# Attention, a SiLU-gated layer and a cosine-gated layer in one kernel: order of stores and loads, place of the sums, and times of two large loads

## The chip, the cores and the metric

The kernel runs on one core of one Trainium2 chip. The metric is the device time of one execution in microseconds (us); the figure for a version is the median of several runs. One further execution was recorded by the hardware profiler, and every row below is read from that one.

## The reference, cut to what matters

Windowed causal attention over 4 batches, 8 heads, 576 positions and head size 64 gives x of 2304 tokens by 512. Two layers follow, all in float32:

```python
x = attn(q, k, v)                       # 2304 x 512
x = (silu(x @ w_gate) * (x @ w_val)) @ w_out      # 512 -> 1536 -> 512
h = x @ w_in2                           # 512 -> 2048
out = (h * cos(h)) @ w_out2             # 2048 -> 512
```

The inputs are 8 bytes wide per element (float64 taken as int64), so each weight has to be turned into float32 on the chip before it is used.

## The kernel before

Each matrix product is made of three matmuls on two-part numbers (a rounded high part and the rest): high by high, high by low, low by high (lines 80 to 82, and 1065 to 1067). So each operand has to be split into `hi` and `lo` first: a cast on ScalarE (ACT) and a subtraction on GpSimd (POOL) or VectorE (DVE).

The program has three stages. In the first, attention runs, and blocks f = 0 to 2 of the first layer's 1536 columns fill gaps of TensorE (PE); their outputs `ye` are stored to `y1d` in DRAM (L270). In the second, the nine blocks f = 3 to 11 run in five groups ([3], [4, 5], ... [10, 11]). A step k is one group's block f on 384 tokens `tb`, and there are 54 steps: six for the first group, twelve for each other. In the third, the second layer runs over 3 parts of 768 tokens by 8 pairs of blocks; each pair is seven products (`prod`, m = 0 to 6) of sums and differences of quarters of tokens and weights, from which four blocks of h are added up (`take`), and rows of the output follow two pairs later.

One step of the second stage does this, engine by engine in this order. PE: 12 matmuls for the gate and 12 for the value of step k (`begin`), then 12 for the output of step k-2 (`second`). ACT: the cast `uh` of step k-1 (L987), SiLU of step k (L978), then whatever `prepare` brings. DVE: the additions to the accumulator `acc` that fall due (L1011, four of them when a group's last block on these tokens is through), `ul` of step k-1 (L989), the product `s` of step k (L980), then `prepare`'s. PSUM has three banks that gate and value take in turn, and five for the output sums.

`prepare(k, count)` runs beside this and makes the weights ready, of both layers. It has three parts. `pipe.scalar` begins `count` items: ACT takes the words of a loaded weight block `st` apart into `cs` (L903, L904). It then casts finished pieces to `hi` (L920 for weights of the first layer, which stay on the chip; L940 for those of the second) and has POOL subtract for `lo` (L921, L941). `pipe.vector` puts float32 together: three operations on DVE (L881 to L883), one on POOL (L885); and for each pair of blocks of `w_in2` it makes four sums of quarters in `sm` (L870 to L873, DVE). `pipe.load` issues the next load of a raw block into `st` (L91, L96) as soon as POOL has let go of its buffer; there are three of these. The pieces of the second layer are not kept: `hi` and `lo` go to DRAM in `wid` and `wod` (L946, L948), and at most three pieces are made in one step, in three buffers each of `sh` and `sl`. These stores are not issued where the piece is made. They are put into a list, and `pipe.start()` of the next step issues them.

All of these DMAs go through SyncE's queue (SP), which issues in program order and waits at each one until its operands are free. So a store that `pipe.start()` issues in step k+1 stands behind the loads of step k.

Before the second stage the program loads `acc` from `y1d`: three loads of up to 768 tokens at L1080, and one of the last 288 tokens at L1086, after the last store of `ye` and ahead of the first `pipe.load()`. At step `CLOSE` (47) whatever is left of the preparation is finished, and the tokens of the third stage's first part are split. At the start of the third stage `load_raw(1)` (L1265) loads the 768 tokens of the second part, 1.5 MB; `make_xt` splits them from pair 2 on. The weights `ws` (L1055) are loaded seven products ahead.

Of the kernel before, what the change touches and what calls it, by code (L numbers as in the profile page):

```python
# [13 lines left out]
ALU = mybir.AluOpType  # L14
# [14 lines left out]
def kernel(  # L29
# [46 lines left out]
    def f32(ap):  # L76
        return ap.bitcast(F32)
# [746 lines left out]
    class Pipe:  # L824
# [3 lines left out]
        def __init__(self):  # L828
            self.todo = []
            for i in range(1, len(groups1)):  # L830
                new = []
                for f in groups1[i]:
                    pool = wa_p if i % 2 else (wa2_p if f == groups1[i][0] else wb_p)
                    for nm, src, col in (("g", w_gate, True), ("v", w_val, True), ("o", w_out, False)):
                        new.append(("w", (i, nm, f), lambda src=src, f=f, col=col: load_stage(src, f, col, stage2), pool))
                old = self.stash(2 * i - 4) + self.stash(2 * i - 3) if i > 1 else []
                self.todo += old[:4] + new + old[4:]
            self.todo += self.stash(6) + self.stash(7)
            self.stages, self.begun, self.ct = [], 0, {}
            self.added = self.done = 0  # L840
            self.logic, self.sums, self.parts, self.outs = [], deque(), deque(), []
            self.kept, self.freed = {}, set()

        def stash(self, p):
# [6 lines left out]
                    ("o", 2 * p, row(2 * p), None), ("o", 2 * p + 1, row(2 * p + 1), None)]  # L851

        def idle(self):
            return self.done == len(self.todo) and not self.outs

        def start(self):
            for fn in self.outs:
                fn()
            self.outs = []

        def load(self):
            while len(self.stages) < min(len(self.todo), self.added + 3):
# [2 lines left out]
        def vector(self):  # L865
            while self.sums:
                n = self.sums.popleft()
                a, b = self.kept.pop(self.todo[n][1]), self.ct[n]
                m = self.kept["m", n] = stash_m.tile([128, 4, 256], F32, tag="sm", name="sm")
                nc.vector.tensor_tensor(out=m[:, 1], in0=b[:, 0:256], in1=b[:, 256:512], op=ALU.add)  # L870
                nc.vector.tensor_tensor(out=m[:, 2], in0=a[:, 0:256], in1=b[:, 0:256], op=ALU.subtract)
                nc.vector.tensor_tensor(out=m[:, 0], in0=m[:, 1], in1=a[:, 0:256], op=ALU.subtract)
                nc.vector.tensor_tensor(out=m[:, 3], in0=a[:, 256:512], in1=m[:, 0], op=ALU.subtract)  # L873
                self.freed.add(n - 1)
                self.parts.extendleft([(n, 3), (n, 2), (n, 1)])
            for n in self.logic:
                kind = self.todo[n][0]
                st, ct = self.stages[n], self.ct[n]
                if wide:
                    ti = ct.bitcast(U32)  # L880
                    nc.vector.tensor_scalar(ct, ct, LEAST_HIGH, GREATEST_HIGH, ALU.max, ALU.min)  # L881
                    nc.vector.tensor_scalar(ti, ti, 3, None, ALU.logical_shift_left)
                    nc.vector.scalar_tensor_tensor(out=ti, in0=st[:, :, 1], scalar=0x80000000, in1=ti,  # L883
                                                   op0=ALU.bitwise_and, op1=ALU.bitwise_or)
                    nc.gpsimd.tensor_tensor(out=ti, in0=ti, in1=st[:, :, 0], op=ALU.add)  # L885
                self.added += 1
                self.stages[n] = None
                if kind == "b":
                    self.sums.append(n)
                else:  # L890
                    self.parts.append((n, 0))
            self.logic = []

        def scalar(self, count, ready):

            for _ in range(count):
                n = self.begun
                if n == len(self.todo) or n >= len(self.stages) or (n >= 5 and n - 5 not in self.freed):
                    break
                ct = self.ct[n] = ct_p.tile([128, 512], F32, tag="cs", name="cs")  # L900
                st = self.stages[n]
                if wide:
                    nc.scalar.activation(out=ct, in_=st[:, :, 1].bitcast(F32), func=AF.Abs, scale=65536.0)  # L903
                    nc.scalar.activation(out=st[:, :, 0], in_=st[:, :, 0], func=AF.Copy, scale=2.0 ** -29)  # L904
                else:
                    nc.scalar.copy(out=ct, in_=st[:, :, 0])
                self.logic.append(n)
                self.begun += 1
            used = 0
            for _ in range(len(self.parts)):  # L910
                n, part = self.parts.popleft()
                kind, key, _, pool = self.todo[n]
                if kind == "w" and not ready(key[0]) or kind != "w" and used == 3:
                    self.parts.append((n, part))
                    continue
                ct = self.ct[n]
                if kind == "w":
                    hi = pool.tile([128, 512], F32R, tag="wh", name="wh")
                    lo = pool.tile([128, 512], F32R, tag="wl", name="wl")
                    nc.scalar.copy(out=hi, in_=ct)  # L920
                    nc.gpsimd.tensor_tensor(out=lo, in0=ct, in1=f32(hi), op=ALU.subtract)  # L921
                    weights[key] = hi, lo
                    self.freed.add(n)
                    self.done += 1
                    continue
                used += 1
                src, w = ct, 512
                if kind == "o":
                    d = wod[key]
                elif part in (1, 2):  # L930
                    src = self.kept["m", n][:, 2 * part - 2:2 * part].rearrange("p s c -> p (s c)")
                    d = wid[key][:, 2 * part:2 * part + 2]
                elif part == 3:
                    src, w, d = ct[:, 256:512], 256, wid[key][:, 6]
                else:
                    d = wid[key][:, 0:2]
                    self.kept[key] = ct
                hi = stash_s.tile([128, 512], F32R, tag="sh", name="sh")[:, :w]
                lo = stash_s.tile([128, 512], F32R, tag="sl", name="sl")[:, :w]
                nc.scalar.copy(out=hi, in_=src)  # L940
                nc.gpsimd.tensor_tensor(out=lo, in0=src, in1=f32(hi), op=ALU.subtract)  # L941

                def out(d=d, halves=(hi, lo), two=kind != "o" and part < 3):
                    for x, t in enumerate(halves):
                        if two:
                            nc.sync.dma_start(out=d[:, :, x], in_=f32(t).rearrange("p (s c) -> p s c", s=2))  # L946
                        else:
                            nc.sync.dma_start(out=d[:, x], in_=f32(t))  # L948
                self.outs.append(out)
                if kind == "o" or part == 3:  # L950
                    self.freed.add(n)
                if part in (0, 3):
                    self.done += 1

    pipe = Pipe()

# [118 lines left out]
    for _ in load0:  # L1075
        pass
    settle()
    for t in range(0, NT - HT, SB):
        e = min(t + SB, NT - HT)
        nc.sync.dma_start(out=acc[:, :, t:e], in_=y1d[:, :, t:e].rearrange("k p t -> p k t"))  # L1080
    i, tb, f = steps[0]
    early = [l1_mms(weights[i, nm, f], *tbs[tb], pl2.tile([128, 512], F32, tag="l2", name="l2")) for nm in ("v", "g")]
    for _ in a_l2(*last[0]):
        flush()
    flush()
    nc.sync.dma_start(out=acc[:, :, NT - HT:], in_=y1d[:, :, NT - HT:].rearrange("k p t -> p k t"))  # L1086
    fa.close()
    cvt.close()
    stage2 = cv.enter_context(tc.tile_pool(name="stage2", bufs=3, side="right", reuse_waits="tile"))
# [13 lines left out]
    def prepare(k, count):  # L1103
        pipe.scalar(count, lambda i: k >= begins[i - 1] + 2)
        pipe.vector()
        pipe.load()

    pipe.load()
    for k in range(K + 1):
        if k < K:  # L1110
            i, tb, f = steps[k]
            while not all((i, nm, f) in weights for nm in "gvo"):
                pipe.start()
                prepare(k, 1)
        late = split(k - 1) if 0 <= k - 1 < K else None
        flush()
# [1 line left out]
            late()  # L1118
        if k == CLOSE:
            while not pipe.idle():  # L1120
                pipe.start()
                prepare(k, 2)
            cv.close()
            xta = pre.enter_context(tc.tile_pool(name="xta", bufs=1, side="right", reuse_waits="tile"))
# [1 line left out]
            load_ws(7)  # L1126
        if k == CLOSE + 1:
            xt_ops = make_xt(0, xta, acc[:, :, 0:SB])
        if k < CLOSE:
            pipe.start()  # L1130
        if k < K:
            begin(k)
        if k < CLOSE:
            prepare(k, 2 if i and k % 2 == 0 and k % 6 != 4 else 1)
        for op in xt_ops[:4]:
            op()
        xt_ops = xt_ops[4:]
# [130 lines left out]
    rows = deque()  # L1268
    bg = deque()
    p7 = None  # L1270
    load_raw(1)
    for k in range(K2 + 2):
        if k >= 2:
            rows += [(k - 2, fi, j) for fi in range(2) for j in range(6)]
        for m in range(7):
# [22 lines left out]
            if m == 1:  # L1298
                load_wo(k - 1 if k else K2)
            s, p = divmod(k, NPAIR)  # L1300
            if m == 3 and s + 1 < NS and p == 2:
                bg += make_xt(s + 1, xta if s % 2 else xtb, raws[s + 1])
            if m == 3 and s + 2 < NS and p == 6:
                load_raw(s + 2)
# [34 lines left out]
```

## Time and profile before

| | us |
|---|---|
| median of 3 runs (1061.98 to 1067.51) | 1065.03 |
| the profiled execution | 1067.15 |
| its span, first to last instruction | 1065.4 |
| PE busy in the span | 1010.7 |
| DVE, ACT, POOL busy | 762.2, 647.6, 485.1 |
| mean granted clock of PE | 0.976 |

A busy PE is not PE at its peak, since matmuls overlap and since the clock is granted in two levels, 2.4 GHz (1.00) and 1.2 GHz (0.50). What counts is where PE has idle time, what released it, and at which clock it went on. The stages are at about 0 to 300, 300 to 675 and 675 to 1062 us of the span.

### The profile page before, as it was taken

The numbers are of one execution on the slowest core, as the hardware profiler recorded it, in microseconds if no ns is written. First come the engines' busy times: TensorE is split into PE (matmuls) and PEld (weight loads), VectorE is DVE, ScalarE is ACT, GpSimd is POOL, SyncE is SP. The second block draws the span as 40 slices with busy tenths as digits, with TensorE's granted clock in tenths as the row PEclk, the third lists the DMA queues.
The fourth block names the chain that finished last, engine by engine and source line by source line (L and its number), as shares of the span: only waits on it lengthen the run. The fifth ranks groups of instructions, "written<-read, shape, count | busy, mean of one in ns | idle before, by whom it ended". The sixth has DMA issues, their size and how long they took to land.

```text
span 1065.4 us, 17549 instructions
## 1 busy us (share of the span) xinstructions
PE 1010.7 (95%) x5796; PEld 949.8 (89%) x5796; DVE 762.2 (72%) x1632; ACT 647.6 (61%) x1438; POOL 485.1 (46%) x553
## 2 busy tenths in 40 slices
PE   7989999999989899898998999899999999999997
PEld 5779999999979899898898899889999889899996
DVE  6897778876148797897796745589766896566664
ACT  5889898984234363453453422387677786686663
POOL 5776577564224474665565532044322452222231
PEclk9999999999989999899999899899999999999999
DMA  5542233312272545555646541566667755575652
GB/s 148 143 112 56 70 72 85 90 29 88 96 248 81 166 150 177 169 178 169 227 122 193 170 149 60 194 221 197 200 218 229 215 185 178 190 244 173 197 178 79
DMA packets 145690, 163.68 MB, mean 154 GB/s; under 512 B 64704, under 2 KB 106688, under 8 KB 145344
## 3 DMA queue, kind: packets, MB, share of 16 engines
q1 hardware_dynamic: 145600, 162.57, 49.3%
q8 instruction: 46, 0.75, 0.3%
q14 instruction: 44, 0.36, 0.1%
HBM read 126.88 MB, written 35.65 MB: 153 GB/s over the span
## 4 chain that ended last, share of the span: by engine, by line
PE 45%; DMA 5%; POOL 3%; DVE 3%; issue 2%; ACT 1%; SPq 1%; POOLq 0%; ACTq 0%; DVEq 0%
PE l L80 8%; PE l L81 8%; PE l L82 8%; PE pm L1065 5%; PE pm L1066 5%; PE pm L1067 5%; POOL cs L885 2%; PE pm L80 2%; PE pm L82 2%; PE pm L81 1%; DMA wid<-sh 1%; POOL sl L941 1%; DMA wod<-sl 1%; DMA wid<-sl 1%; DMA ws<-wid 1%
## 5 line engine op out<-in xcount | busy, mean ns | idle before, releaser
L1189 POOL TENSOR_TENSOR r<-r,c 128x384 f32<-128x384 f32 x96 | 105.5, 1099 | 263.2 <-ACT r L1187 176.4
L80 PE MATMUL pm<-xh,wh 128*128 128x384 f32 (+1 forms) x452 | 152.2, 337 | 2.3 <-ACT s L978 2.3
L81 PE MATMUL pm<-xl,wh 128*128 128x384 f32 (+1 forms) x452 | 146.6, 324 | 0.0
L82 PE MATMUL pm<-xh,wl 128*128 128x384 f32 (+1 forms) x452 | 146.6, 324 | 0.0
L81 PE MATMUL l<-wo,hh 128*128 128x512 f32 x288 | 113.1, 393 | 0.0
L80 PE MATMUL l<-wo,hh 128*128 128x512 f32 x288 | 113.1, 393 | 0.0
L82 PE MATMUL l<-wo,hl 128*128 128x512 f32 x288 | 112.9, 392 | 0.0
L885 POOL TENSOR_TENSOR cs<-cs,st 128x512 uint32<-128x512 uint32 x56 | 81.8, 1465 | 64.6 <-DVE cs L883 50.3
L1065 PE MATMUL pm<-xh,ws 128*128 128x384 f32 x318 | 107.5, 338 | 0.0
L1066 PE MATMUL pm<-xl,ws 128*128 128x384 f32 x318 | 107.4, 338 | 0.0
L1067 PE MATMUL pm<-xh,ws 128*128 128x384 f32 x318 | 107.3, 337 | 0.0
L581 POOL TENSOR_SCALAR e<-e,st 128x256 f32<-128x256 f32 (+1 forms) x144 | 68.5, 487 | 72.3 <-DVE st L576 38.8
L80 PEld LDWEIGHTS pm<-xh,wh 128*128 128x128 f32 x452 | 86.6, 192 | 3.2 <-ACT s L978 3.2
L81 PEld LDWEIGHTS pm<-xl,wh 128*128 128x128 f32 x452 | 86.8, 192 | 0.0
L82 PEld LDWEIGHTS pm<-xh,wl 128*128 128x128 f32 x452 | 86.2, 191 | 0.0
L80 PE MATMUL l<-uh,wh 128*128 128x384 f32 x216 | 75.0, 347 | 11.0 <-DVE acc L1011 10.9
L1179 ACT ACTIVATE a<-c 128x384 f32<-128x384 f32 x96 | 49.8, 518 | 57.7 <-DVE c L1205 57.7
L989 DVE TENSOR_TENSOR ul<-s,uh 128x384 fp32r<-128x384 f32 x54 | 42.7, 791 | 52.9 <-ACT uh L987 52.8
L1184 DVE SCALAR_TENSOR_TENSOR r<-a,r 128x384 f32<-128x384 f32 x96 | 74.4, 775 | 3.3
L1186 ACT ACTIVATE r<-r 128x384 f32<-128x384 f32 x96 | 50.3, 524 | 40.4 <-DVE r L1184 40.4
L82 PE MATMUL l<-uh,wl 128*128 128x384 f32 x216 | 74.2, 343 | 0.0
L81 PE MATMUL l<-ul,wh 128*128 128x384 f32 x216 | 74.2, 343 | 0.0
(199 smaller groups left out, 2934.6 us busy)
## 6 DMA issues: line engine op xcount, KB each, us to landing
ws<-wid SPq DMA_DIRECT2D x168, 256.0 KB, 2.9
wo<-wod SPq DMA_DIRECT2D x48, 512.0 KB, 4.9
st<-in_moe_w_out_dram SPq DMA_DIRECT2D x28, 512.0 KB, 3.6
st<-in_moe_w_in_dram SPq DMA_DIRECT2D x16, 512.0 KB, 4.0
st<-in_moe_w_gate_dram SPq DMA_DIRECT2D x12, 512.0 KB, 3.9
st<-in_moe_w_val_dram SPq DMA_DIRECT2D x12, 512.0 KB, 4.4
wid<-sh SPq DMA_DIRECT2D x24, 256.0 KB, 4.6
wid<-sl SPq DMA_DIRECT2D x24, 256.0 KB, 4.8
```

What stands on the lines that cost most here:

```text
L80: nc.tensor.matmul(out=ps, lhsT=ah, rhs=bh, start=start, stop=False)
L81: nc.tensor.matmul(out=ps, lhsT=ah, rhs=bl, start=False, stop=False)
L82: nc.tensor.matmul(out=ps, lhsT=al, rhs=bh, start=False, stop=stop)
L581: nc.gpsimd.tensor_scalar(e[:, :w], e[:, :w], st[:, 6 + m:7 + m], 1.0, ALU.mult, ALU.mult)
L885: nc.gpsimd.tensor_tensor(out=ti, in0=ti, in1=st[:, :, 0], op=ALU.add)
L1065: nc.tensor.matmul(out=o, lhsT=wh, rhs=xh_, start=start and kk == 0, stop=False, skip_group_check=True)
L1066: nc.tensor.matmul(out=o, lhsT=wh, rhs=xl_, start=False, stop=False, skip_group_check=True)
L1067: nc.tensor.matmul(out=o, lhsT=wl, rhs=xh_, start=False, stop=kk == 1, skip_group_check=True)
L1179: nc.scalar.activation(out=a, in_=h, func=AF.Copy, scale=INV2PI, bias=MAGIC)
L1184: nc.vector.scalar_tensor_tensor(out=r, in0=a, scalar=-C2, in1=r, op0=ALU.mult, op1=ALU.add)
L1186: nc.scalar.activation(out=r, in_=r, func=AF.Abs)
L1189: nc.gpsimd.tensor_tensor(out=r, in0=r, in1=h, op=ALU.mult)
```

## The change

Five things change. The stores of `hi` and `lo` of a step are issued within the same `pipe.scalar`, all `hi` first, then all `lo`, and so ahead of the loads of that step. The four sums of quarters go from DVE to POOL. `acc` is loaded in three equal parts: the first before the second stage as it was, the others in steps 0 and 2, after `begin`. Two items instead of one are begun in every fourth step (from step 8 on: 10 steps) instead of in two of three even steps (14 steps). In the third stage `load_raw(1)` is issued at pair 1, product 3, and `make_xt` of a next part begins at pair 3 instead of 2.

```diff
         def idle(self):
-            return self.done == len(self.todo) and not self.outs
-
-        def start(self):
-            for fn in self.outs:
-                fn()
-            self.outs = []
+            return self.done == len(self.todo)
...
-                nc.vector.tensor_tensor(out=m[:, 1], in0=b[:, 0:256], in1=b[:, 256:512], op=ALU.add)
-                nc.vector.tensor_tensor(out=m[:, 2], in0=a[:, 0:256], in1=b[:, 0:256], op=ALU.subtract)
-                nc.vector.tensor_tensor(out=m[:, 0], in0=m[:, 1], in1=a[:, 0:256], op=ALU.subtract)
-                nc.vector.tensor_tensor(out=m[:, 3], in0=a[:, 256:512], in1=m[:, 0], op=ALU.subtract)
+                nc.gpsimd.tensor_tensor(out=m[:, 1], in0=b[:, 0:256], in1=b[:, 256:512], op=ALU.add)
+                nc.gpsimd.tensor_tensor(out=m[:, 2], in0=a[:, 0:256], in1=b[:, 0:256], op=ALU.subtract)
+                nc.gpsimd.tensor_tensor(out=m[:, 0], in0=m[:, 1], in1=a[:, 0:256], op=ALU.subtract)
+                nc.gpsimd.tensor_tensor(out=m[:, 3], in0=a[:, 256:512], in1=m[:, 0], op=ALU.subtract)
...
-                def out(d=d, halves=(hi, lo), two=kind != "o" and part < 3):
-                    for x, t in enumerate(halves):
-                        if two:
-                            nc.sync.dma_start(out=d[:, :, x], in_=f32(t).rearrange("p (s c) -> p s c", s=2))
-                        else:
-                            nc.sync.dma_start(out=d[:, x], in_=f32(t))
-                self.outs.append(out)
+                for x, t in enumerate((hi, lo)):
+                    if kind != "o" and part < 3:
+                        outs.append((x, d[:, :, x], f32(t).rearrange("p (s c) -> p s c", s=2)))
+                    else:
+                        outs.append((x, d[:, x], f32(t)))
                 if kind == "o" or part == 3:
                     self.freed.add(n)
                 if part in (0, 3):
                     self.done += 1
+            for x, dst, src in sorted(outs, key=lambda o: o[0]):
+                nc.sync.dma_start(out=dst, in_=src)
...
-    for t in range(0, NT - HT, SB):
-        e = min(t + SB, NT - HT)
-        nc.sync.dma_start(out=acc[:, :, t:e], in_=y1d[:, :, t:e].rearrange("k p t -> p k t"))
+
+    def load_acc(s):
+        c = slice(s * SB, (s + 1) * SB)
+        nc.sync.dma_start(out=acc[:, :, c], in_=y1d[:, :, c].rearrange("k p t -> p k t"))
+
+    load_acc(0)
...
-    nc.sync.dma_start(out=acc[:, :, NT - HT:], in_=y1d[:, :, NT - HT:].rearrange("k p t -> p k t"))
...
-        if k < CLOSE:
-            pipe.start()
         if k < K:
             begin(k)
+        if k in (0, 2):
+            load_acc(1 + k // 2)
         if k < CLOSE:
-            prepare(k, 2 if i and k % 2 == 0 and k % 6 != 4 else 1)
+            prepare(k, 2 if i and k % 4 == 0 else 1)
...
-    load_raw(1)
     for k in range(K2 + 2):
...
+            if k == 1 and m == 3:
+                load_raw(1)
-            if m == 3 and s + 1 < NS and p == 2:
+            if m == 3 and s + 1 < NS and p == 3:
                 bg += make_xt(s + 1, xta if s % 2 else xtb, raws[s + 1])
```

## Rows read from the trace of the kernel before

**Rows 1.** The profile's first part: busy time, share of the span, instructions, of PE.
```profile
PE 1010.7 (95%) x5796; PEld 949.8 (89%) x5796; DVE 762.2 (72%) x1632; ACT 647.6 (61%) x1438; POOL 485.1 (46%) x553
```

**Rows 2.** Busy time by stretches: length, PE, PEld, DVE, ACT, POOL, clock, DMA share, GB/s.
```profile
300.00:675.00 375.00, 349.62 (x1908) 345.53 (x1907) 278.67 (x432) 157.85 (x298) 184.38 (x132) 0.95 0.48 155
675.00:1065.00 390.00, 381.15 (x1885) 342.90 (x1884) 270.49 (x453) 268.02 (x533) 120.94 (x104) 0.99 0.61 197
...
685.00:694.00 9.00, 5.94 (x20) 5.69 (x19) 5.01 (x9) 6.72 (x14) 2.62 (x4) 0.62 0.81 296
```

**Rows 3.** Who waited for whom, PE, 290 to 690 us: total, times, longest.
```profile
PE l L80 <- ACT s L978: 12.1, 4, 5.1
PE l L80 <- DVE acc L1011: 10.9, 4, 4.2
PE l L1065 <- DMA ws<-wid: 3.1, 1, 3.1
```

**Rows 4.** Timeline of DVE, products `s` of steps 2, 47, 53: start, us, instruction, idle before.
```profile
315.30 0.56 DVE L980 TENSOR_TENSOR s<-s,l 128x384 f32<-128x384 f32 x1 [0.41 <-PE l L82]
...
633.26 0.56 DVE L980 TENSOR_TENSOR s<-s,l 128x384 f32<-128x384 f32 x1 [3.13 <-PE l L82]
...
671.06 0.56 DVE L980 TENSOR_TENSOR s<-s,l 128x384 f32<-128x384 f32 x1 [3.13 <-PE l L82]
```

**Rows 5.** Who waited for whom, 300 to 675 us, ACT's casts for the stores.
```profile
ACT sh L940 <- DMA wid<-sh: 62.9, 21, 9.0
...
ACT sh L940 <- DMA wod<-sh: 22.3, 5, 9.2
```

**Rows 6.** Timelines of ACT, POOL and SP around one wait, 353 to 375 us.
```profile
353.44 1.13 ACT L940 CAST sh<-sm 128x512 fp32r<-128x512 f32 x2
...
370.07 0.62 ACT L940 CAST sh<-cs 128x512 fp32r<-128x512 f32 x1 [9.01 <-DMA wid<-sh]
...
360.54 3.08 POOL L885 TENSOR_TENSOR cs<-cs,st 128x512 uint32<-128x512 uint32 x2
...
363.64 0.37 SPq L91 DMA_DIRECT2D st<-in_moe_w_gate_dram  x1
364.07 0.50 SPq L946 DMA_DIRECT2D wid<-sh  x1
```

**Rows 7.** Groups by shape, 300 to 632 us (busy, mean ns, idle); last, min/median/max ns.
```profile
L885 POOL TENSOR_TENSOR cs<-cs,st 128x512 uint32<-128x512 uint32 x56 | 81.8, 1465 | 64.6 <-DVE cs L883 50.3 <-issue 5.5 <-ACT s L978 4.5
...
L941 POOL TENSOR_TENSOR sl<-cs,sh 128x256 fp32r<-128x256 f32 x8 | 8.0, 1002 | 9.4 <-DMA wod<-sl 4.9 <-DMA wid<-sl 4.4
...
L882 DVE TENSOR_SCALAR cs<-cs 128x512 uint32<-128x512 uint32 x56 | 43.6, 778 | 1.9
...
L870 DVE TENSOR_TENSOR sm<-cs x8: 410/426/1500, 349.4 to 606.2; 128x256 f32<-128x256 f32 x8
```

**Rows 8.** The profile's DMA issues: count, KB each, median us to landing.
```profile
ws<-wid SPq DMA_DIRECT2D x168, 256.0 KB, 2.9
...
st<-in_moe_w_gate_dram SPq DMA_DIRECT2D x12, 512.0 KB, 3.9
...
wid<-sh SPq DMA_DIRECT2D x24, 256.0 KB, 4.6
```

**Rows 9.** Timelines of SP and ACT where the second stage begins, 282 to 313 us.
```profile
296.63 3.90 SPq L270 DMA_DIRECT2D y1d<-ye  x4
302.84 0.37 SPq L1086 DMA_DIRECT2D acc<-y1d  x1
...
309.01 0.66 ACT L903 ACTIVATE cs<-st 128x512 f32<-128x512 f32 x1 [9.64 <-DMA st<-in_moe_w_gate_dram]
```

**Rows 10.** Timelines of SP, ACT and PE where the third stage begins, 678 to 698 us.
```profile
680.53 0.36 SPq L1265 DMA_DIRECT2D raw<-y2d  x1
...
690.64 0.48 ACT L1215 COPY q<-l 128x384 f32<-128x384 f32 x1 [2.05 <-PE l L1067]
...
697.81 0.44 PE L1065 MATMUL l<-xh,ws 128*128 128x384 f32 x1 [0.46 <-DVE c L1205]
```

More of the change, by code (lines that the diff above doesn't have):

```diff
@@ L840, in __init__ @@
             self.added = self.done = 0
-            self.logic, self.sums, self.parts, self.outs = [], deque(), deque(), []
+            self.logic, self.sums, self.parts = [], deque(), deque()
             self.kept, self.freed = {}, set()
@@ L908, in scalar @@
                 self.begun += 1
-            used = 0
+            used, outs = 0, []
             for _ in range(len(self.parts)):
@@ L1120 @@
             while not pipe.idle():
-                pipe.start()
                 prepare(k, 2)
@@ L1128 @@
             xt_ops = make_xt(0, xta, acc[:, :, 0:SB])
-        if k < CLOSE:
-            pipe.start()
         if k < K:
             begin(k)
+        if k in (0, 2):
+            load_acc(1 + k // 2)
         if k < CLOSE:
-            prepare(k, 2 if i and k % 2 == 0 and k % 6 != 4 else 1)
+            prepare(k, 2 if i and k % 4 == 0 else 1)
         for op in xt_ops[:4]:
```

## The prediction

> **What bounds the kernel now.** The page's first part comes first: PE is busy 95% of the span [rows 1]. The work for PE is the same after the change, so all that can be won is its idle time and its time at the lower clock. The busy time by stretches says where that lies: in the second stage PE idles 375 - 349.6 = 25.4 us and its granted clock is 0.95 on average, which takes (1 - 0.95) x 375 = 19 us away, a part of it while PE idled anyway. The third stage has 8.9 us of idle time, of which the last few are the drain, and a clock of 0.99 [rows 2]. The view of waits names the releasers: PE waited 12.1 us for SiLU on ACT, 10.9 us for the additions to `acc` on DVE, 3.1 us for a load of `ws` [rows 3].
>
> How much is lost in all is read from the pace. From step 47 to step 53 no preparation runs, and `s` comes every (671.06 - 633.26)/6 = 6.30 us. From step 2 to step 53 it takes 355.8 us, and 51 steps at 6.30 are 321.3 [rows 4]. So 34.5 us are lost behind step 2, idle time and low clock together (pot B). Ahead of it lies one wait of 5.1 us [rows 3], with, as an estimate, some 2 us lost to the low clock behind it (in the whole stage 19 us of clock stand beside 25 of idle time): about 7 (pot A). At the start of the third stage lie 3.1 us of waiting and at most (1 - 0.62) x 9 = 3.4 us of clock [rows 2, 3] (pot C). The most that can be won is 34.5 + 7 + 6.5 = 48 us.
>
> Why ACT and DVE are late is in their own waits: ACT's casts waited 62.9 + 22.3 = 85 us for stores of `sh` made a step before [rows 5]. ACT works in order, so `uh` and SiLU stand behind such a cast; DVE's `ul` and `s`, and its additions, stand behind those. One case in full [rows 6]: two casts are made at 353.4. Their stores could go by 355, but SP holds the loads of that step first, and the last of those waits for POOL's two L885, which end at 363.62. The load is issued at 363.64, the first store at 364.07, nine microseconds late. The next cast needs that buffer, waits 9.0 us and runs at 370.07. PE stands still soon after.
>
> **Stores ahead of loads.** Nothing is added but the order. Stores `hi` wait for ACT's casts, stores `lo` for POOL's subtractions, and both come before the L885 for which the loads wait anyway, so the loads lose only SP's time for issuing: up to six stores at the 0.50 us of a row, 3 us [rows 6]. With three loads ahead in flight and 3.9 us to land [rows 8] that lies beside other work; ACT would wait behind it if POOL fell a step behind. A store of `hi` takes 4.6 us to land [rows 8]. Issued right after its cast it is down well before the same place of the next step, 6.30 us later. So pot B loses its main cause. In the case above, a store that leaves nine microseconds sooner ends a wait of 9.0 us to nothing.
>
> **Fewer double steps.** 14 become 10. By the program's order all 56 items still are begun by step 45; the last piece falls into `CLOSE` itself, with one cast that waits for no late store. Before, the last piece was made in step 44. I cost it at 0 to 2 us, taken as 0: step 47 has no other preparation.
>
> **Sums on POOL.** DVE loses 8 x 4 operations; one takes 0.41 us at best and 1.5 us at worst, median 0.43 [rows 7]: about 1.7 us for a pair of blocks, 14 in all. POOL gets them. No row shows such a sum on POOL; the nearest is the 128x256 subtraction, same two inputs, 1.00 us; the 128x512 one of L885 takes 1.47 [rows 7]. Bounds for a pair: 4 x 0.43 = 1.7 (as fast as DVE) and 4 x 1.47 = 5.9; I take 4.0, from the row of the same shape. On average there is room: POOL is busy 184 us of 375 [rows 2], and 184 + 32 = 216 in some 335 would be 65%. In bursts there is little. In steps 16 to 21 the changed program begins 8 items, makes 10 pieces of 512 columns and two of 256, and sums two pairs: 18 x 1.47 + 2 x 1.0 + 8 = 36 us in 6 x 6.30 = 37.8. Steps 27 to 32 come to 35, steps 38 to 43 to 34 by the same count. Behind a sum on POOL's queue stand the L885 of the step, the loads that wait for these, and the next step's `lo`. POOL and DVE also hold each other up: L870 takes 0.41 us alone and up to 1.5 beside POOL, L882 0.78 on average [rows 7]. So I don't give all of pot B back: 27 of 34.5, the remaining 7.5 for the three bursts. Bounds: 15 (stores still decide half of it) to 34.5.
>
> The row of this case has the subtraction at 1.00 us on POOL against 0.43 on DVE [rows 7]. The Trainium skill, GPSIMD Engine Reference, section Engine selection, advises against this very move: elementwise work on two tensors belongs on VectorE, and GpSimd is about twice as slow. By that rule, trace agreeing (2.3 times), a move of elementwise work to POOL costs time; here that would only show if POOL became the bound, which is the third rival below.
>
> **`acc` in three parts.** Before, the last load of `acc` waited for the last `ye` store and was issued at 302.84, and the first raw block got its place in the queue behind it; ACT's L903 waited for that block until 309.01, 9.6 us, with `uh` and SiLU of step 1 behind it [rows 9]. After, the block can be issued when the stores of `ye` have been, at 296.63 + 3.90 = 300.53 [rows 9]. With 3.9 us to land [rows 8] it is there at about 304.4, 4.6 us sooner. PE's wait shrinks from 5.1 to about 0.5, and the clock may stay up. Of pot A I take 6 back (4.5 to 7). The parts loaded in steps 0 and 2 are first added to in steps 5 and 7, more than 20 us later; what they cost is a place ahead of the later raw loads, at two issues nothing that I can price above 1 us.
>
> **Raw tokens later.** At 680.53 the 1.5 MB load goes ahead of the `ws` loads [rows 10], and PE waits 3.1 us for one of them [rows 3]. Without it a `ws` load lands in 2.9 us [rows 8], and it is asked for as soon as the product seven places ahead is through, some 7 us before its own (1.05 us a product, worked out below). So this wait goes. What is next is ACT. A pair has 21 operations on ACT at about the 0.48 us of a row [rows 10], 10 us, and its seven products, six matmuls each, take PE 42/36 x 6.30 = 7.4 us, as long as no output rows lie between (the first two pairs). While PE stood, ACT had work: it waited for PE only 2.05 us [rows 10]. So the matmul at 697.81, which waited for DVE behind ACT [rows 10], can come at most about 2 us sooner, and PE then waits in front of it instead. A wait of that length lowers the clock again. I take 1 of pot C, bounds -2 and 6.5. The load itself comes at pair 1, ahead of `ws` needed some 12 us later, and `make_xt` at pair 3 still ends before pair 8 needs it: nothing.
>
> **The sum.** Against the profiled execution's 1067.15 (a span of 1065.4 and 1.75 around it): 1067.15 - 6 - 27 - 1 = 1033. That execution lies 2.1 us above the median of 1065.03, so on the median's scale the forecast is 1031.
>
> **The rivals.**
>
> Partial relief, 0.17. The stores leave sooner but three buffers are still too few, or a load of the step before holds SP. For it: many stores took more than the median to land, since they go in sixes. Against: 6.30 us between uses. Price: half of pot B stays, 1065 - 6 - 15 - 1 = 1043.
>
> POOL takes ACT's place, 0.13. If pieces and sums run 20% over their rows' means, because POOL and DVE hold each other up more, the three bursts come to 44, 42 and 41 us instead of 37.8: 6 + 4 + 3 = 13 lost, and with the low clock behind each such wait about 20. 1065 - 6 - 34.5 + 20 + 3 (steps 8 to 10) is about 1048.
>
> The same place on the other side, slower than before, 0.03: the changes other than the sums bring some 35 us, and 5 more are needed to be measurably slower, so the 8 groups of sums would have to cost PE 5 us each. The bursts leave about 1.4 us of slack for each group; so a sum would have to take (4.0 + 1.4 + 5)/4 = 2.6 us. The row says 1.00. The time would be about 1071.
>
> The stores don't in fact pass the loads, or another wait of the same length takes their place: about 1062, 0.03.
>
> All of it, pot C too: 1065 - 48 = 1017 to 1022, 0.04.
>
> **How the numbers follow.** The forecast has 0.60, between 1023 and 1039. The range of 1021 to 1048 takes in partial relief and half of the POOL case and leaves about 0.18 out. What a measurement can tell from no change here is about 0.5%, 5 us. Faster: 0.60 + 0.17 + 0.13 + 0.04 = 0.94; the same 0.03; slower 0.03.
>
> **What would show it.** Right: `s` from step 2 to 53 at 6.4 to 6.5 us a step; ACT's wait for `sh` stores under 25 us; L903's first wait near 5 us; no wait for `ws` near 690 but one for DVE in its place, some microseconds later; mean clock near 0.99. The POOL case would show as PE waiting for DVE or ACT whose own chain ends at L870 to L885 on POOL in steps 16 to 21 and 27 to 32. The prediction is wrong if ACT's casts still wait for stores, if a sum on POOL takes over 1.5 us, or if a new wait stands where raw loads are late.

## The result, and the profile after

The changed kernel takes 1025.96 us (median; 1025.35 to 1027.21) against 1064.97 us before: a ratio of 0.9636, with a 95% interval of 0.9609 to 0.9663. It is 39 us faster. The profiled execution took 1027.21 us with a span of 1025.4, 40.0 us less than before's. Its line numbers lie a little lower: L898 is L903 of before, L935 and L936 are L940 and L941, L972 SiLU, L974 the product `s`, L880 POOL's part of the preparation, L1005 the additions to `acc`, L947 the stores of `hi` and `lo`. Every kernel below has its own line numbers, shifted by its edit.

Busy time by stretches, the second and the third stage of the changed kernel (length, PE, PEld, DVE, ACT, POOL, clock, DMA share, GB/s):

```profile
300.00:635.00 335.00, 334.33 (x1910) 333.76 (x1909) 280.58 (x399) 160.12 (x300) 213.81 (x164) 1.00 0.56 178
635.00:1025.00 390.00, 381.79 (x1896) 343.77 (x1894) 272.47 (x455) 268.61 (x534) 119.62 (x104) 0.99 0.61 198
```

The second stage answers to the first line of [rows 2]: PE idles 0.7 us instead of 25.4, its clock is at 1.00 instead of 0.95, and the stage is 40 us shorter. The third stage is what it was, to within 2 us. Who waited for whom, PE, 290 to 690 us, answering to [rows 3]:

```profile
PE l L1059 <- DVE c L1199: 4.0, 2, 3.6
PE l L80 <- ACT s L972: 0.7, 1, 0.7
```

The waits for `acc` and for `ws` are gone. One wait is left, of 3.6 us, at the start of the third stage, where before had 3.1 us for `ws`. The pace, answering to [rows 4], is read from DVE's timeline (steps 2, 47 and 53):

```profile
312.16 0.55 DVE L974 TENSOR_TENSOR s<-s,l 128x384 f32<-128x384 f32 x1
...
595.15 0.56 DVE L974 TENSOR_TENSOR s<-s,l 128x384 f32<-128x384 f32 x1 [2.74 <-PE l L82]
...
632.95 0.56 DVE L974 TENSOR_TENSOR s<-s,l 128x384 f32<-128x384 f32 x1 [3.13 <-PE l L82]
```

Steps 2 to 53 take 320.8 us, where 51 undisturbed steps at 6.30 us take 321.3; before it was 355.8. That is 35.0 of the 40 us. From step 0 to step 2 it is 10.3 us instead of 15.2 (`s` of step 0 at 301.90, before at 300.09): 4.9 more. From step 53 to the end it is 392.5 instead of 394.3: 1.8. The first stage took 1.8 us longer in this execution, which makes up the difference; in the traces of this document `s` of step 0 comes at anything from 296.9 to 302.2 us, so this lies within what that stage varies by.

And the cause that was named, ACT's casts waiting for stores ([rows 5]; 300 to 635 us here):

```profile
ACT sh L935 <- POOL cs L880: 4.8, 5, 1.6
...
ACT sh L935 <- DMA wid<-sh: 1.7, 1, 1.7
```

85 us of such waits became 1.7. How that comes about is seen in the timelines of ACT, then SP, in steps 8 and 9, the place that answers to [rows 6]:

```profile
354.36 1.12 ACT L935 CAST sh<-sm 128x512 fp32r<-128x512 f32 x2
...
360.72 1.14 ACT L935 CAST sh<-cs 128x512 fp32r<-128x512 f32 x2
...
355.36 0.34 SPq L96 DMA_DIRECT2D st<-in_moe_w_out_dram  x1
355.75 1.58 SPq L947 DMA_DIRECT2D wid<-sh  x3
357.43 2.27 SPq L947 DMA_DIRECT2D wid<-sl  x3
360.87 0.37 SPq L91 DMA_DIRECT2D st<-in_moe_w_gate_dram  x1
```

The casts are made at 354.36 and their stores leave at 355.75, right behind a load of the step before that POOL released at 355.36 (its L880 of 353.82 takes 1.51 us). In the kernel before, the same stores left 10.6 us after their casts began; here it is 1.4 us. The next casts run at 360.72 and wait for nothing.

### The profile page after: what moved, and what is told of

It is laid out like the page before. It is cut to its first block, busy times and chain, and to the rows that moved or that the text cites. A ratio compares the mean times of both kernels' runs of the same rounds, so it can differ in the third digit from the quotient of the medians.

```text
span 1025.4 us, 17616 instructions
## 1 busy us (share of the span) xinstructions
PE 997.0 (97%) x5796; PEld 938.7 (92%) x5796; DVE 765.1 (75%) x1600; ACT 648.9 (63%) x1438; POOL 512.6 (50%) x585
## 4 chain that ended last, share of the span: by engine, by line
PE 88%; ACT 6%; issue 2%; DVE 2%; DMA 1%; POOL 1%; SPq 0%; POOLq 0%; ACTq 0%; DVEq 0%
PE l L80 13%; PE l L81 13%; PE l L82 13%; PE pm L80 7%; PE pm L82 7%; PE pm L81 7%; PE pm L1059 5%; PE pm L1060 5%; PE pm L1061 5%; PE pv L658 3%; PE t L591 2%; PE s L523 2%; ACT e L565 2%; PE pq L426 1%; PE s L80 1%
## 5 line engine op out<-in xcount | busy, mean ns | idle before, releaser
L80 PE MATMUL pm<-xh,wh 128*128 128x384 f32 (+1 forms) x452 | 149.9, 332 | 0.0
L880 POOL TENSOR_TENSOR cs<-cs,st 128x512 uint32<-128x512 uint32 x56 | 80.9, 1445 | 55.1 <-DVE cs L878 47.5
L1178 DVE SCALAR_TENSOR_TENSOR r<-a,r 128x384 f32<-128x384 f32 x96 | 76.8, 800 | 3.3
L565 ACT ACTIVATE e<-e,st 128x256 f32<-128x256 f32 (+1 forms) x144 | 68.0, 475 | 9.4 <-DVE st L556 8.6
L80 PE MATMUL l<-uh,wh 128*128 128x384 f32 x216 | 72.9, 337 | 0.0
```

Of the source, the lines that this page charges most:

```text
L80: nc.tensor.matmul(out=ps, lhsT=ah, rhs=bh, start=start, stop=False)
L565: nc.scalar.activation(out=e[:, :w], in_=e[:, :w], func=AF.Exp, bias=st[:, m:m + 1], scale=-1.0, accum_out=st[:, 2 + m:3 + m])
L1178: nc.vector.scalar_tensor_tensor(out=r, in0=a, scalar=-C2, in1=r, op0=ALU.mult, op1=ALU.add)
```

## The experiments

"Lost" below is the time from `s` of step 2 to `s` of step 53, less 321.3 us. Like 321.3, it is read from one profiled execution of each kernel. All ratios are to the kernel before, measured beside it.

| kernel | median us | ratio, 95% | lost, us |
|---|---|---|---|
| before | 1065 | | 34.5 |
| changed | 1025.96 | 0.9636 (0.9609 to 0.9663) | -0.5 |
| changed, again | 1025.46 | 0.9627 (0.9602 to 0.9652) | 0.0 |
| stores_only | 1036.44 | 0.9738 (0.9703 to 0.9774) | 5.7 |
| old_stores | 1048.63 | 0.9851 (0.9813 to 0.9888) | 23.8 |
| sums_dve | 1026.24 | 0.9647 (0.9612 to 0.9682) | 0.6 |
| doubles14 | 1028.27 | 0.9666 (0.9625 to 0.9708) | 0.1 |
| old_acc | 1031.90 | 0.9684 (0.9662 to 0.9707) | 1.6 |
| raw_early | 1024.68 | 0.9629 (0.9603 to 0.9655) | 0.1 |
| sums_twice | 1031.40 | 0.9681 (0.9662 to 0.9699) | 4.4 |
| sums_x3 | 1057.61 | 0.9929 (0.9908 to 0.9951) | 31.9 |
| cast_pool | 1026.23 | 0.9638 (0.9613 to 0.9662) | 0.1 |
| take_first | 1025.86 | 0.9623 (0.9604 to 0.9643) | -0.9 |
| chains_held | 1021.13 | 0.9599 (0.9578 to 0.9621) | -0.4 |

**The order of the stores, alone and alone undone.** stores_only is the kernel before with the first of the five changes alone: the list and `pipe.start()` go, and each step issues its own stores, all `hi` first.

> The kernel before with one edit, the stores issued within their own step; sums on VectorE, 14 double steps, the loads of acc and of the raw tokens as before. Theory A (the order of stores is the cause of nearly all that the second stage lost): the 34.5 us behind step 2 come back almost whole, while the first wait of 5 us and the one for ws near 690 stay; 1032 to 1038 us. Theory B (relief of VectorE and fewer double steps carry a large share, since PE also waited 10.9 us for VectorE's additions): under half comes back, 1045 to 1055 us, with PE still waiting for acc.

1036.4 us, within theory A's range: 28.7 of the 34.5 us come back by the order alone. No run separates the earlier issue from the order `hi` before `lo`. ACT's casts (300 to 660 us) wait 2.3 us for stores instead of 85:

```profile
ACT sh L935 <- DMA wod<-sh: 2.0, 1, 2.0
...
ACT sh L935 <- DMA wid<-sh: 0.3, 1, 0.3
```

Who waited for whom, PE, 290 to 690 us:

```profile
PE l L80 <- ACT s L972: 5.1, 1, 5.1
PE l L80 <- DVE acc L1005: 4.0, 5, 1.5
PE l L1059 <- DMA ws<-wid: 3.4, 1, 3.4
```

The first and third lines are waits that this part doesn't touch. The second is most of what is left of the stage's loss: five short waits for DVE, none over 1.5 us. The other way round, old_stores is the changed kernel with the list and `pipe.start()` put back.

> The changed kernel with the stores put back into a list that the next step issues; the four other edits stay. Theory A: ScalarE's casts wait for stores again, 60 us or more in all, PE waits for SiLU and additions, 1050 to 1060 us. Theory B: the other edits hold what they won, 1035 to 1045 us.

1048.6 us, a little under theory A's range and above theory B's. The waits of ACT's casts, 300 to 670 us, then PE's:

```profile
ACT sh L940 <- DMA wid<-sh: 52.0, 19, 8.6
...
ACT sh L940 <- DMA wod<-sh: 4.9, 4, 3.3
```

```profile
PE l L80 <- DVE acc L1011: 9.4, 6, 3.5
PE pm L80 <- ACT s L978: 4.3, 3, 2.0
PE l L1065 <- DVE c L1209: 4.0, 2, 3.6
PE l L80 <- ACT s L978: 3.6, 3, 2.1
```

The casts wait 57 us instead of 85, and 23.8 us are lost instead of 34.5. So the other changes aren't worth nothing: while the stores are late, they soften it by 10.7 us. This run has them all together, so it doesn't say which of them does it; sums and schedule are the two that take work or double steps from the stage. Theory A holds for the main part, and not for "nearly all".

**Sums and schedule, each undone.** sums_dve writes `nc.vector` for `nc.gpsimd` in the four sums; doubles14 restores `2 if i and k % 2 == 0 and k % 6 != 4 else 1`.

> The changed kernel with the four sums of quarters back on VectorE. Theory A: VectorE has room for 14 us more, 1025 to 1028 us, no wait of PE comes back. Theory B: PE waits for VectorE's additions to acc again in steps 8 to 45, 1032 us or more.

> The changed kernel with the schedule of 14 double steps of before. Theory A: 1025 to 1029 us, pace of s still under 6.4 us a step. Theory B: double steps that follow each other make VectorE and GpSimd late, PE waits 5 us or more, 1034 us or more.

Neither loses anything that can be seen in its trace: 0.6 and 0.1 us behind step 2. Without both, stores_only loses 5.7. That suggests that each covers for the other, but no run undoes just these two: stores_only lacks the parts of `acc` as well, and a kernel that lacks nothing but those (old_acc, below) loses 1.6 us behind step 2. So about 4 us, as much as the five waits for DVE, are left for sums and schedule together. doubles14's median is 2.3 us higher than the changed kernel's and the intervals overlap; its trace is of the fastest of its four executions (1024.33 us), so what the others lost isn't seen.

**How much POOL bears.** Each line of the four sums stands twice in sums_twice, three times in sums_x3; the values are the same.

> The changed kernel with each sum of quarters on GpSimd made twice, so 7 us a pair of blocks. By the count of GpSimd's work in the three bursts (42, 41 and 39 us against 37.8): 8 us lost behind step 2, some low clock, 1033 to 1038 us. If a loss grows from the first microsecond of sums on GpSimd, half of what three times cost (32 us over two added rounds): 1040 to 1043 us.

> The changed kernel with each sum of quarters on GpSimd made three times in a row (the result is the same), so a pair of blocks costs GpSimd about 10.5 us instead of 3.5, which is 2.6 us a sum, the point from which the prediction's slower rival was to decide. By the count of that rival (GpSimd has 1 to 4 us of slack in a burst of six steps): the three bursts come to 49, 48 and 46 us against 37.8, 30 us lost and more by the low clock, 1058 to 1070 us. By the theory that the buffers between GpSimd and PE take up most of it (three raw loads, five cs, three pieces): 1035 to 1050 us.

Once costs nothing, twice 4.4 us, three times 31.9. That isn't a loss that grows in proportion from the first microsecond. It looks like one that begins near the point where POOL's work in a burst of six steps passes the steps' own 37.8 us. The count of the prediction with the durations after (1.45 for 512 columns, 0.96 for 256, 3.5 for a group of sums) gives 35.0, 33.6 and 32.1 us for once, none over; 42.0, 40.6 and 39.1 for twice, 8 us over in sum where 4.4 were lost; for three times 49, 48 and 46, 29 us over where 31.9 were lost, low clock included. So nothing was lost at 85 to 93% of the 37.8 us by this count, and 4.4 us at 103 to 111%; where between them the loss begins wasn't measured. Nor does the count hit the trace. From `s` of step 16 to `s` of step 22, the sums made once, twice and three times (length, PE, PEld, DVE, ACT, POOL, clock, DMA share, GB/s):

```profile
399.56:439.96 40.40, 40.40 (x232) 40.29 (x231) 38.73 (x48) 20.72 (x40) 33.07 (x26) 1.00 0.69 222
396.28:439.14 42.86, 40.60 (x232) 40.28 (x231) 38.46 (x49) 20.52 (x39) 38.63 (x34) 1.00 0.61 196
399.82:449.77 49.95, 41.91 (x226) 40.76 (x225) 38.42 (x48) 20.46 (x40) 44.53 (x43) 0.91 0.53 174
```

POOL is busy 33.1, 38.6 and 44.5 us, 2 to 5 us less than the count has. In the changed kernel it is DVE, at 38.7 of 40.4 us, that is nearer to its limit there. PE's waits in sums_x3 (290 to 690 us) are for DVE, not for POOL itself:

```profile
PE l L80 <- DVE acc L1013: 19.1, 9, 5.1
PE pm L80 <- ACT s L980: 4.2, 2, 2.5
```

Behind them stand ACT's casts, which wait for POOL's sums (300 to 660 us; L873 and L876 are the last of the third and fourth sum):

```profile
ACT sh L943 <- POOL sm L873: 26.1, 6, 8.3
ACT sh L943 <- POOL sm L876: 16.0, 8, 2.4
```

By time, sums_x3 lies half a microsecond below the range expected by that count, and well over the other theory's. sums_twice, at 1031.4 us, lies under the ranges of both theories: the count foretold 1033 to 1038.

**The loads of `acc`.** old_acc restores the loads at L1080 and L1086 of before and drops those of steps 0 and 2.

> The changed kernel with the accumulators loaded before the second stage, the last load behind the last store of ye, as before. If the first wait was caused by that load's place in the queue: PE's wait near 310 us is 5 us again instead of 0.7, with the lower clock behind it, 1030 to 1033 us. If the raw block would have landed late anyway: 1026 to 1028 us.

1031.9 us, 6 us more than the changed kernel (1025.96, again 1025.46), as expected for a load whose place in the queue matters. PE's wait at the start is back (PE's waits, 290 to 690 us):

```profile
PE l L80 <- ACT s L972: 4.8, 1, 4.8
```

From step 0 to step 2 its trace takes 14.9 us instead of 10.3. The low clock that follows the wait goes on behind step 2, whose `s` is at 311.87. By stretches, with the columns of the lines above, old_acc has a granted clock of 0.61 from 312 to 314 us, and the changed kernel 1.00:

```profile
312.00:314.00 2.00, 2.00 (x9) 2.00 (x8) 1.97 (x3) 0.62 (x1) 2.00 (x3) 0.61 0.36 92
...
312.00:314.00 2.00, 2.00 (x13) 2.00 (x13) 1.97 (x4) 0.71 (x3) 2.00 (x2) 1.00 0.85 283
```

So a part of what the first wait costs, up to the 1.6 us of old_acc, is counted as lost behind step 2, in the kernel before and in stores_only too.

**The raw tokens.** raw_early restores `load_raw(1)` ahead of the loop and `p == 2`; changed, again is the changed kernel beside it.

> The changed kernel as it is, to stand beside the next kernels on the same chip: 1026 us, a wait of PE of 3 to 4 us for VectorE at about 20 us behind the last step of the second stage, none for ws.

> The changed kernel with the load of the raw tokens at the start of the third stage and their split from pair 2, as before. Theory A (behind the wait for ws stands ScalarE's chain, so little is won by taking the wait away): 1 to 3 us more, 1027 to 1029 us; PE waits 3 us for ws and only about 0.5 us for VectorE afterwards. Theory B (the load was the bound of the start): 5 us more or above, 1031 us.

1024.7 against 1025.5 us: no difference, and below the ranges of both theories. PE's waits in raw_early, 290 to 690 us:

```profile
PE l L1059 <- DMA ws<-wid: 2.4, 1, 2.4
PE l L80 <- ACT s L972: 0.8, 1, 0.8
PE l L1059 <- DVE c L1199: 0.8, 2, 0.5
```

A wait of 2.4 us for `ws` stands where the changed kernel has 3.6 for DVE. Moving the load exchanged one for the other.

**What stands behind the wait that is left.** Three edits of the first pairs of the third stage. cast_pool moves eight casts from ACT to POOL:

```diff
-        nc.scalar.copy(out=hi, in_=r)
+        if k < 2:
+            nc.gpsimd.tensor_scalar(hi, r, 1.0, 0.0, ALU.mult, ALU.add)
+        else:
+            nc.scalar.copy(out=hi, in_=r)
```

> The changed kernel with one edit: for the first two pairs of the third stage the cast to the high part of h cos h is done by GpSimd, which is idle there, instead of ScalarE; eight operations of 0.5 us leave ScalarE. Theory A (PE's wait of 3.6 us is ScalarE's backlog of the first two pairs): that wait shrinks by 1.5 to 3 us and the time by 1 to 4 us, 1022 to 1025 us. Theory B (the chain's latency or VectorE decides): no change, 1026 us, the wait stays over 3 us.

```profile
PE l L1059 <- DVE c L1202: 4.7, 2, 4.4
```

The wait grew from 3.6 to 4.4 us (the larger of the two in that line), the time stayed. So taking work off ACT alone doesn't help. But this doesn't rule ACT out: in the 18 us up to PE's restart DVE waited for ACT 1.5 us instead of 2.5, but its own operations took longer beside POOL's casts (one L1178 1.29 us instead of 0.56), 16.1 us busy instead of 14.3. take_first calls `take(k, m, ps)` before `slot_chains()` for k < 2.

> The changed kernel with one edit: in the first two pairs of the third stage, the addition that frees a product's PSUM bank stands ahead of the cosine chains' operations of the same slot on VectorE and ScalarE, instead of behind them. Theory A (PE's wait of 3.6 us is for an addition that stands on VectorE behind operations which wait for ScalarE and GpSimd): the wait goes or falls under 1 us and 3 to 5 us are saved, 1021 to 1023 us. Theory B (VectorE and ScalarE have more work in the first two pairs than PE, so the wait only moves to a later product): 1024 to 1027 us, a wait of 2 us or more some products later.

1025.9 us, with the same wait of 3.6. The timelines show why it tells nothing of either theory: up to 5 us behind PE's wait DVE and ACT execute the same operations in the same order as in the changed kernel. A chain's first step came after its own addition and before the next one already; the calls were exchanged, not the order. chains_held does change it: the four chains of pair 1 start one slot after another in pair 2.

```diff
+            if k == 2 and held:
+                live.append(held.popleft())
             slot_chains()
...
                 take(k, m, ps)
+            if k == 1 and m in (1, 4, 5, 6):
+                held.append(live.pop())
```

> The changed kernel with the four cosine chains of pair 1 held back until pair 2, where output rows give PE more work, so that in pair 1 the additions that free PSUM banks no longer stand behind those chains' operations on VectorE. Theory A (the order on VectorE decides): the addition for product 4 of pair 1 comes 2 us sooner, PE's wait of 3.6 us falls to 1 to 2 us, 1023 to 1025 us. Theory B (the work of ScalarE and VectorE in the first pairs exceeds PE's, whatever the order): the wait shrinks but another of about the same length stands in pair 2 or 3, 1025 to 1028 us.

```profile
PE l L1059 <- DVE c L1199: 2.4, 2, 2.1
```

The wait falls from 3.6 to 2.1 us, a little over theory A's 1 to 2, and no other wait follows up to 700 us. The addition had stood on DVE behind the operations of a chain that waited 0.9 us for ACT, and holding the chain back frees it. In the 2.1 us that are left DVE waits for nothing: from 652 to 654 us, while PE stands, it is busy all the time, with sums of other products and operations of other chains. From step 53 to the end it is 391.0 us instead of 392.5 (393.4 in the changed kernel's other trace). The median of 1021.1 is the lowest of all, but its ratio of 0.9599 (0.9578 to 0.9621) overlaps with the changed kernel's 0.9627 (0.9602 to 0.9652) measured with as many rounds, and it lies under theory A's range, so that it beats the changed kernel is likely, not shown.

## Why the prediction was right, point by point

1031 us was forecast with a range of 1021 to 1048, and 1026 measured. The sum had 34 us to win against the profiled execution; its spans differ by 40: 35.0 behind step 2, 4.9 ahead of it, 1.8 in the third stage, less the 1.8 by which the first stage ran longer.

**Pot B, sized at 34.5.** Right as a pot: 35.0 us came back, and `s` comes every 6.29 us, under the 6.4 to 6.5 that was named as a sign of being right. The forecast gave 27 of them, and this is the term that was mis-sized. The 7.5 us held back were for POOL's three bursts. Two things made that too much. A group of sums takes 3.5 us on POOL, not 4.0 (means of 0.85, 0.96, 0.84 and 0.87 us; below, from the tile's own view, min/median/max ns):

```profile
L865 POOL TENSOR_TENSOR sm<-cs x8: 737/770/1188, 346.6 to 585.9; 128x256 f32<-128x256 f32 x8
L866 POOL TENSOR_TENSOR sm<-cs x8: 732/988/1194, 347.3 to 587.0; 128x256 f32<-128x256 f32 x8
L867 POOL TENSOR_TENSOR sm<-sm,cs x8: 727/742/1192, 348.3 to 587.7; 128x256 f32<-128x256 f32 x8
L868 POOL TENSOR_TENSOR sm<-cs,sm x8: 734/833/1074, 349.1 to 588.5; 128x256 f32<-128x256 f32 x8
```

And the prediction's own count, 36, 35 and 34 us in 37.8, said that POOL would get through. These shares of 90 to 95% were charged as if they cost something; sums made once show that here they cost nothing. The measured sums lie on the side of the subtraction that was taken as the nearest row, somewhat under its 1.00 us.

**Its cause, the stores.** Right: 28.7 us by the order alone. What the prediction didn't say is that the other changes together are worth 10.7 us without it and 5.7 beside it, of which up to 1.6 belong to the first wait, and that sums and schedule are worth nothing that can be measured singly. "Partial relief" did not come: a store still leaves behind a load of the step before, but within 1.4 us of its cast (354.36 and 355.75 above), and with three buffers ACT waits 1.7 us in all.

**Fewer double steps, costed at nothing.** Right as far as the traces show: the changed kernel has no loss at step 47, and the old schedule loses 0.1 us.

**Pot A, 6 of 7.** Right: 4.9 us between steps 0 and 2 by the traces, about 6 by the times of old_acc, which take in the low clock behind step 2. The first raw block was forecast to be issued right behind the `ye` stores and to land 3.9 us later. SP, then ACT:

```profile
298.43 3.90 SPq L270 DMA_DIRECT2D y1d<-ye  x4
302.38 0.43 SPq L91 DMA_DIRECT2D st<-in_moe_w_gate_dram  x1
...
306.34 0.66 ACT L898 ACTIVATE cs<-st 128x512 f32<-128x512 f32 x1 [5.16 <-DMA st<-in_moe_w_gate_dram]
```

ACT's wait is 5.2 us instead of 9.6 [rows 9], and PE's 0.7, where 0.5 had been worked out.

**Pot C, 1 of 6.5.** Half right in reason, and its size can't be told from nothing: the third stage took 1.8 us less in one trace and 0.9 in the other, and 2.4 less with the load at its old place (raw_early, 391.9 us). The wait for `ws` went and a wait behind DVE came, for the same product as before, as said [rows 10]. That product starts 24.1 us behind `s` of step 53, where before it was 26.8, so 2.7 us sooner instead of at most about 2:

```profile
657.02 0.45 PE L1059 MATMUL l<-xh,ws 128*128 128x384 f32 x1 [3.63 <-DVE c L1199]
```

raw_early shows that the move is worth nothing that can be measured. But the step "What is next is ACT" isn't borne out: with eight operations less on ACT the wait got longer. Where the addition stands on DVE matters, as chains_held shows; but holding the chains back also takes their operations on ACT out of pair 1, so ACT's share in the 3.6 us stays open.

**The rivals.** POOL taking ACT's place, and the same place on the slower side, were priced by the count of POOL's work. That count gets the order right, and the amount for three times (29 counted, 31.9 lost), but not for twice (8 and 4.4). The point given for the slower side, 2.6 us a sum, is what sums_x3 makes: the kernel is then still 0.7% faster than before (0.9929), since the other changes bring 39 us and not 35, and the sums cost 32 us and not 40. The sums did move to the slower engine: 3.3 us a group by the medians against 1.7 on DVE, 3.5 against 2.1 by the means. That agrees with the rule of the Trainium skill (GPSIMD Engine Reference, section Engine selection) that the prediction quotes, and yet the move cost no time that can be measured (1025.96 and 1026.24 us).

## What to carry to other kernels

Here a store issued late, behind a load that waited, held up the engine that needed the store's buffer, and cost 28.7 us of 1065. So look for casts or copies that wait for their own stores of a step earlier, and issue the store where its data is made. Work that was moved to a less busy engine cost nothing while that engine's counted work in the fullest six steps stayed at 85 to 93% of their time, and began to cost something by 103 to 111%; so count it burst by burst rather than by the average, and then read the busy time from the trace. A wait for a load that ends shortly before another engine would have been late anyway was worth nothing here (2.4 us for `ws` became 3.6 for DVE): look for the next wait of the same group before counting it.

## What the runs showed of the hardware that was not expected

Moving the sums off DVE did not make DVE less busy. The cleanest pair is the changed kernel and sums_dve, which differ in nothing else and run at the same pace: from 350 to 580 us DVE is busy 209.1 us without the sums and 208.9 with them. Its three operations of the preparation took 753, 778 and 948 ns before (L882 in [rows 7]; beside it, 300 to 632 us):

```profile
L883 DVE SCALAR_TENSOR_TENSOR cs<-st,cs 128x512 uint32<-128x512 uint32 x56 | 53.1, 948 | 1.9
...
L881 DVE TENSOR_SCALAR cs<-cs 128x512 f32<-128x512 f32 x56 | 42.2, 753 | 11.4 <-ACT cs L903 11.4
```

After (295 to 600 us):

```profile
L878 DVE SCALAR_TENSOR_TENSOR cs<-st,cs 128x512 uint32<-128x512 uint32 x56 | 63.0, 1126 | 1.9
...
L877 DVE TENSOR_SCALAR cs<-cs 128x512 uint32<-128x512 uint32 x56 | 50.9, 909 | 1.9
...
L876 DVE TENSOR_SCALAR cs<-cs 128x512 f32<-128x512 f32 x56 | 48.8, 872 | 4.6 <-ACT cs L898 4.6
```

That is 0.43 us more for each of 56 items, 24 us in all, and more than the 32 sums had kept DVE busy (17 us by their means, where the prediction had 14 by the medians): DVE is busy 765.1 us of the span, before 762.2, with fewer operations. With the sums back on DVE the three take 781, 836 and 1123 ns, and with nothing but the stores changed (stores_only, 295 to 610 us) 754, 905 and 1052. So 0.23 to 0.26 us of it come without any sum on POOL, and some 0.17 us with them. More sums on POOL add little: made three times (295 to 640 us), the three take 868, 866 and 1159 ns. That DVE and POOL meet more often at the faster pace would explain it, but no run shows that.
